# A second level of the seven-product form in four products of a tiled MLP, with its factors made in flight and streamed in 256 KB pieces

## The chip, the cores and the metric

One core of a Trainium2 chip runs the whole program in one launch. The metric is the device time in microseconds (us), smaller is better. Engines are named as in the profile: PE (TensorE, matmuls), DVE (VectorE), ACT (ScalarE), POOL (GpSimd), SP (SyncE). POOL and SP are used here almost only to issue DMA transfers.

## The reference

Lightning attention (batch 4, 8 heads, 768 positions, head size 64), then an MLP on each of the 3072 tokens:

```python
# attention, by blocks of positions, with a decay per head (lam)
intra = ((qb @ kb.T) * Dmask) @ vb
inter = (qb * lam_pow) @ kv_state
out   = intra + inter
kv_state = lam_block * kv_state + (kb * rev_pow).T @ vb
# MLP: x is 3072 x 512, w_in 512 x 2048, w_out 2048 x 512
h = x @ w_in
g = h - tanh(h)
return g @ w_out
```

Everything is fp32. The MLP dominates the arithmetic.

## The kernel before

**Groups.** The tokens are taken in six groups of 512: 128 positions of each of the four batches. The state of the attention runs from group to group. For each group there are two halves of attention work (batches 0, 1 and 2, 3), each with the steps `att_transpose` (L252), `att_scores` (L273), `att_out` (L309) and `att_state` (L287). At the end `att_sums` (L337) makes the sums of x that the MLP needs. From group 1 on, the attention of group g+1 runs in pieces between the products of group g, so that its waits lie beside TensorE work.

**Group 0** runs the MLP plainly (`up_plain` L481, `down_plain` L496) while the weights come in and are rounded (`round_block` L218). With each block of w_out `sums_out` (L207) forms seven factors from its four quadrants on DVE, and POOL stores them to a DRAM tensor `factors` (L215, L216), eight pairs of stores in all; the last is issued at 153.87 us.

**Groups 1 to 5** use the seven-product form of Strassen and Winograd: a product of two matrices, each cut in quadrants, is made of seven half-size products and some sums instead of eight. In the first stage, `up(g, u, n)` (L392) does product n of a quarter u (0 to 3) of the 2048 hidden columns, four matmuls of 128x256 each; its factors sit in SBUF. `evict` (L367) combines the products with ACT copies and DVE additions, and applies tanh. In the second stage, `down(g, n)` (L434) does product n over the whole hidden dimension, 16 matmuls of 128x256, with a factor of w_out of 1 MB that is streamed from `factors`. `load_factor` (L424) issues that load on POOL's queue, two products ahead, into a ring of two 1 MB buffers (pool `wst`, tag `w`).

**Order.** The main loop (L548 to L569) is an order written out by hand: for each u products 2, 6, 5, 7, then the next u's product 1 (or product 1 of the second stage after the last), then 4 and 3. In the second stage 2, 6, 5, 7, then the next group's first product, 4, 3. The first-half attention steps stand among u = 2, u = 3 and the second stage's product 2; the second half's stand after products 6, 5 and 7. Each engine takes its instructions in order, so a DVE operation that waits holds back those written after it; some operations are pinned with `keep_in_program_order`, and a scheduler places the others by what they need. Product 3 of the last group is split in three so that the end is short (L444 to L451).

**Loads on SP.** For groups 2 and up, q and k are loaded as blocks that DVE can transpose (L146): for each of the eight tiles, q and k of four batches, 16 transfers of 16 KB, hence 128 a group, into eight buffers of the pool `late`. k and v are loaded also in natural order (L125, `load_natural`), 256 KB each. These loads are issued a group ahead of use, as soon as their buffers are free; SP's queue holds them in the order q, k of batch 0, q, k of batch 1 and so on. The pool `late` is opened before group 1 in place of the staging pool of the weights (L546, L547).

**Stores.** The results of a group leave by four stores of 256 KB on POOL's queue (L476).

[...]

Of the kernel before, what the change touches and what calls it, by code (L numbers as in the profile page):

```python
# [16 lines left out]
BLK = 128  # L17
# [6 lines left out]
def kernel(  # L24
# [48 lines left out]
    wst = ctx.enter_context(tc.tile_pool(name="wst", bufs=2))  # L73
# [3 lines left out]
    gpool = ctx.enter_context(tc.tile_pool(name="gpool", bufs=NU))  # L77
# [3 lines left out]
    stage_open = tc.tile_pool(name="stage", bufs=1)  # L81
    stage = stage_open.__enter__()
# [37 lines left out]
    def load_natural(g, b, names):  # L120
        for name, src, bufs in (("q", q, 2), ("v", v, 4), ("k", k, 3)) if (g, b) == (0, B - 1) else (
                ("q", q, 2), ("k", k, 3), ("v", v, 4)):
            if name in names:
                x = io.tile([128, H, D], F32, name=f"{name}_nat", tag=name, bufs=bufs)
                nc.sync.dma_start(out=x, in_=src[b, :, ts(g, BLK), :].rearrange("h s d -> s h d"))  # L125
                raw[g, b][name] = x

    def load(n):

        while at["loaded"] < min(n, len(chunks)):
            g, b = chunks[at["loaded"]]
            if g < GB:
                raw[g, b] = {}
                load_natural(g, b, "qkv")
                at["loaded"] += 1
                continue
            for b in range(B):
                raw[g, b] = {}  # L140
                for name, src in (("q", q), ("k", k)):
                    x = late["pool"].tile([128, NP, BLK // 32, 32], F32, name=f"{name}_blk", tag="blk", bufs=2 * B)
                    for p in range(NP):
                        for c in range(4):
                            blk = src[b, 2 * p + c // 2, ts(g, BLK), ts(c % 2, 32)]
                            nc.sync.dma_start(out=x[ts(c, 32), p], in_=blk.rearrange("(r t) a -> t r a", t=32))  # L146
                    raw[g, b][name + "b"] = x
            for b in range(B):
                load_natural(g, b, "kv" if g < NG - 1 else "v")
            at["loaded"] += B  # L150
# [207 lines left out]
    def product_bank(key, n):  # L358

        if n == 1:  # L360
            banks[key, "y"] = bank("y", "y", 2)
# [5 lines left out]
    def evict(key, n, dst, finish):  # L367

        y, z, w = (banks.get((key, x)) for x in "yzw")
        end = key == ("down", NG - 1)  # L370
        halves = [slice(0, 256), slice(256, 512)] if end else [slice(None)]
# [7 lines left out]
        elif n == 7:  # L379
            for x in halves:  # L380
                nc.scalar.activation(dst(22)[:, x], y[:, x], AF.Copy)  # L381
            nc.vector.tensor_tensor(dst(22), dst(22), z, op=AL.add)  # L382
            finish(22, dst(22))
            if end:
                nc.vector.tensor_tensor(dst(12), dst(12), z, op=AL.add)
# [6 lines left out]
    def up(g, u, n):  # L392
        a, bname = FACT[n]
        wt = {"A11": w1[u][:, 0:2, 0], "A12": w1[u][:, 2:4, 0], "S3": w1[u][:, 0:2, 1], "A22": w1[u][:, 2:4, 1],
              "S1": ws[u][:, 0], "S2": ws[u][:, 1], "S4": ws[u][:, 2]}[a]
        x = xt[g][bname] if bname != "B11" else xt[g, 0][:, 0:2]
        t, first = product_bank(("up", g, u), n)
        for m in range(2):
            for kt in range(2):
                nc.tensor.matmul(out=t[:, m, :], lhsT=wt[:, kt, ts(m, 128)], rhs=x[:, kt, :],  # L400
                                 start=first and m == 0 and kt == 0, stop=kt == 1, skip_group_check=True)

        def dst(c):
            if (g, u, c) not in hid:
                hid[g, u, c] = gpool.tile([128, 2 * HB], F32, name=f"g{c}", tag=f"g{c}")
            return hid[g, u, c]

        def finish(c, src):
            th = work.tile([128, 2 * HB], F32, name="th", tag="th")
            nc.scalar.activation(th, src, AF.Tanh)  # L410
            nc.vector.tensor_tensor(dst(c), src, th, op=AL.subtract)  # L411

        evict(("up", g, u), n, dst, finish)
        if n == 3:

            hid[g, u, "S1"] = gpool.tile([128, 2 * HB], F32, name="gs1", tag="gs1")
            nc.vector.tensor_tensor(hid[g, u, "S1"], dst(12), dst(22), op=AL.add)
            nc.vector.tensor_tensor(dst(12), dst(11), dst(12), op=AL.subtract)

    ORDER = (1, 2, 6, 5, 7, 4, 3)  # L420
    stream = [(g, n) for g in range(1, NG) for n in ORDER]
    sent = {"n": 0}

    def load_factor(n):  # L424

        while sent["n"] < min(n, len(stream)):
            key = stream[sent["n"]]
            blks[key] = wst.tile([128, KH, 256], F32, name="wb", tag="w")
            nc.gpsimd.dma_start(out=blks[key], in_=factors[XAT[FACT[key[1]][1]]])  # L429
            sent["n"] += 1  # L430

    HIDAT = {"A11": 11, "A12": 21, "A22": 22, "S1": "S1", "S2": 11, "S3": 12, "S4": 21}

    def down(g, n):  # L434
        load_factor(stream.index((g, n)) + 2)
        wb = blks.pop((g, n))
        c = HIDAT[FACT[n][0]]

        def hidden(kt, m):
            return hid[g, kt // 2, c].rearrange("q (m c) -> q m c", m=2)[:, kt % 2, ts(m, 128)]  # L440

        if g == NG - 1 and n == 3:

            rows = out.rearrange("(b s) d -> s b d", b=B)[ts(g, BLK), 0:2, 256:512]  # L444
            for tag, bufs, m, c0, c1 in (("w", 1, 0, 0, 256), ("z", 1, 1, 0, 128), ("y", 2, 1, 128, 256)):
                t = bank("end", tag, bufs)[:, 0:c1 - c0]
                for kt in range(KH):
                    nc.tensor.matmul(out=t, lhsT=hidden(kt, m), rhs=wb[:, kt, c0:c1], start=kt == 0, stop=kt == KH - 1)  # L448
                o = hid[g, 12].rearrange("q (m c) -> q m c", m=2)[:, m, c0:c1]
                nc.vector.tensor_tensor(o, o, t, op=AL.add)  # L450
                nc.sync.dma_start(out=rows[:, m, c0:c1], in_=o)  # L451
            return
        t, first = product_bank(("down", g), n)
        for m in range(2):
            for kt in range(KH):
                a = hidden(kt, m)
                nc.tensor.matmul(out=t[:, m, :], lhsT=a, rhs=wb[:, kt, :], start=first and m == 0 and kt == 0,  # L457
                                 stop=kt == KH - 1, skip_group_check=True)
        if n == 2:
            for u in range(NU):  # L460
                nc.vector.tensor_tensor(hid[g, u, 11], hid[g, u, "S1"], hid[g, u, 11], op=AL.subtract)
            for u in range(NU):
                nc.vector.tensor_tensor(hid[g, u, 21], hid[g, u, 21], hid[g, u, 11], op=AL.subtract)

        def dst(c):
            if (g, c) not in hid:
                hid[g, c] = opool.tile([128, 512], F32, name=f"o{c}", tag="o")
            return hid[g, c]

        def finish(c, src):  # L470
            i, j = divmod(c - 11, 10)
            if src is not dst(c):
                nc.vector.tensor_copy(dst(c), src)
            rows = out.rearrange("(b s) d -> s b d", b=B)[ts(g, BLK), 2 * i:2 * i + 2, ts(j, 256)]
            o = dst(c).rearrange("q (m c) -> q m c", m=2)
            nc.gpsimd.dma_start(out=rows, in_=o)  # L476

        evict(("down", g), n, dst, finish)


    def up_plain(u, c):  # L481
        a, t = divmod(c - 11, 10)
        h = bank("h", *(("y", 2) if t == 0 else ("z", 1) if a == 0 else ("w", 1)))
# [5 lines left out]
        th = work.tile([128, 2 * HB], F32, name="th", tag="th")  # L489
        nc.scalar.activation(th, h, AF.Tanh)  # L490
        hid[0, u, c] = gpool.tile([128, 2 * HB], F32, name=f"g{c}", tag=f"g{c}")
        nc.vector.tensor_tensor(hid[0, u, c], h, th, op=AL.subtract)
# [3 lines left out]
    def down_plain(kt):  # L496
        wt = pair[kt]
        for b in range(B):
            if kt == 0:
                obank[b] = bank("op0", *((("y", 2), ("y", 2), ("z", 1), ("w", 1))[b]))  # L500
            i, t = divmod(b, 2)
            for a in range(2):
                g = hid[0, kt // 2, 11 + i + 10 * a].rearrange("q (m c) -> q m c", m=2)[:, kt % 2, ts(t, 128)]
# [42 lines left out]
    stage_open.__exit__(None, None, None)  # L546
    late["pool"] = ctx.enter_context(tc.tile_pool(name="late", bufs=8))  # L547
    up(1, 0, 1)  # L548
    for g in range(1, NG):
        last = g == NG - 1  # L550
        p0, p1 = attention(g + 1) if not last else ([], [])
        for u in range(NU):
            for n in (2, 6, 5, 7):
                up(g, u, n)
            if u + 1 < NU:
                up(g, u + 1, 1)
            else:
                down(g, 1)
# [4 lines left out]
        for n, more in ((2, p0[2:]), (6, p1[0:1]), (5, p1[1:2]), (7, p1[2:])):  # L563
            down(g, n)
            run(more)
        if not last:
            up(g + 1, 0, 1)
        down(g, 4)
        down(g, 3)  # L569
# [30 lines left out]
```

## Time and profile before

| what | us |
|---|---|
| median of 3 runs | 692.55 (691.5 to 692.83) |
| profiled execution, its own time | 693.28 |
| its span, first to last instruction | 691.4 |
| DVE, ACT, POOL busy | 353.2, 167.9, 55.8 |
| product 2 of the first quarter starts at (groups 1 to 4) | 157.65, 266.83, 376.00, 485.18 |
| a group, first to first | 109.2 |
| POOL, 35 factor loads of 1 MB, issue to landing (median) | 5.7 |
| POOL, 19 stores of 256 KB, issue to landing (median) | 5.5 |

The profile is one execution. "Span" lies between its first and last instruction. A busy share is of the span. The "chain that ended last" is followed back from the last instruction, at each step to what released it; a time on it is time that the kernel could be shorter only if that piece were shorter, or its cause. Each line of a chain has a start, a duration, an engine, the tile that is written, the source line and the count of instructions. An issue line of a queue has a start, a duration, and the number of transfers; a bracket behind it is a wait and what ended it. A matmul in fp32 leaves two records. Matmuls' names are those of the program's tiles: `wb` a streamed factor, `g` hidden values, `sp` scores, `kv` the state's update, `op` attention's output.

### The profile page before, as it was taken

Reading aid. Unit: us, or ns where it says so; the run is one execution under the profiler, and the core shown is the slowest. Engines: PE = TensorE matmul, PEld = TensorE weight load, DVE = VectorE, ACT = ScalarE, POOL = GpSimd, SP = SyncE. Lnnn points to the kernel's source line nnn. Section 1 sums busy time; section 2 is a strip of 40 time slices with the busy share of each in tenths; the row PEclk is TensorE's granted clock in tenths of the full one; section 3 lists DMA queues with packets and bytes.
Section 4 is the critical chain, followed back from the end, with each engine's and each line's share of the span. In section 5 each row is a group of like instructions: output and inputs, shape, how many; then the busy total and the mean of one; then the engine's idle time right before and its main releaser. Section 6 shows DMA issues by size and latency. Waiting matters only on the chain.

```text
span 691.4 us, 10409 instructions
## 1 busy us (share of the span) xinstructions
PE 678.4 (98%) x4112; PEld 569.2 (82%) x4112; DVE 353.2 (51%) x608; ACT 167.9 (24%) x283; POOL 55.8 (8%) x96
## 2 busy tenths in 40 slices
PE   6899999999999999999999999999999999999998
PEld 5688855558888888888888888888888888888887
DVE  3798756993467332566441446713446712254501
ACT  2665433323321011331010332000332101233100
POOL 0001212120001001000111000001000001000101
PEclk9999999999999999999999999999999999999999
DMA  9869948556227646263655803455600332400342
GB/s 188 215 201 252 286 151 242 180 167 172 35 33 178 163 131 180 34 112 92 169 170 141 157 1 87 104 163 175 159 1 1 131 129 80 149 1 0 100 159 106
DMA packets 144143, 89.82 MB, mean 130 GB/s; under 512 B 129824, under 2 KB 130208, under 8 KB 139616
## 3 DMA queue, kind: packets, MB, share of 16 engines
q0 software_dynamic: 11232, 58.46, 24.7%
q1 hardware_dynamic: 132720, 30.71, 23.2%
q8 instruction: 32, 0.52, 0.3%
q14 instruction: 15, 0.12, 0.1%
q10 hardware_dynamic: 144, 0.00, 0.0%
HBM read 75.50 MB, written 13.63 MB: 129 GB/s over the span
## 4 chain that ended last, share of the span: by engine, by line
PE 94%; DMA 3%; DVE 2%; ACT 0%; issue 0%; SPq 0%; ACTq 0%; DVEq 0%
PE y L457 20%; PE y L400 20%; PE z L400 10%; PE z L457 9%; PE op L504 8%; PE h L487 6%; PE w L457 5%; PE w L400 5%; PE sp L280 3%; PE op L331 3%; DMA raw<-in_moe_w_in_dram 2%; PE op L325 1%; PE kv L300 1%; PE tp L265 1%; PE end L448 1%; DMA q_nat<-in_q_dram 1%
## 5 line engine op out<-in xcount | busy, mean ns | idle before, releaser
L457 PE MATMUL y<-wb,g 128*128 128x256 f32 x640 | 142.3, 380 | 0.7 <-ACT o L381 0.7
L457 PEld LDWEIGHTS y<-wb,g 128*128 128x128 f32 x640 | 120.9, 190 | 18.1 <-ACT o L381 1.1
L400 PE MATMUL y<-xt,w 128*128 128x256 f32 x320 | 73.6, 380 | 0.0
L410 ACT ACTIVATE th<-g 128x512 f32<-128x512 f32 x60 | 37.8, 630 | 140.7 <-DVE g L375 86.1
L400 PEld LDWEIGHTS y<-xt,w 128*128 128x128 f32 x320 | 60.5, 190 | 8.9 <-issue 0.6
L411 DVE TENSOR_TENSOR g<-g,th 128x512 f32<-128x512 f32 x60 | 41.4, 690 | 32.5 <-ACT th L410 32.5
L429 POOL DMA_DIRECT2D wb<-factors x35 | 19.0, 543 | 481.0 <-PE y L457 364.9
L487 PE MATMUL h<-xt,w 128*128 128x256 f32 x256 | 56.2, 381 | 0.9 <-DVE w L237 0.9
L284 DVE TENSOR_TENSOR ss<-sp,mask 128x512 f32<-128x512 f32 x48 | 30.8, 684 | 51.4 <-PE sp L280 51.4
L504 PE MATMUL op<-wt,g 128*128 128x512 f32 x128 | 56.5, 595 | 0.0
L487 PEld LDWEIGHTS h<-xt,w 128*128 128x128 f32 x256 | 48.3, 190 | 8.3 <-DVE w L237 1.3
L504 PEld LDWEIGHTS op<-wt,g 128*128 128x128 f32 x128 | 23.8, 190 | 27.7 <-issue 27.0
L382 DVE TENSOR_TENSOR g<-g,z 128x512 f32<-128x512 f32 x20 | 13.7, 686 | 49.9 <-ACT g L381 49.9
L400 PE MATMUL y<-tt,ws 128*128 128x256 f32 x160 | 37.8, 379 | 0.0
L400 PE MATMUL w<-xt,w 128*128 128x256 f32 x160 | 37.8, 379 | 0.0
L400 PE MATMUL z<-tt,ws 128*128 128x256 f32 x160 | 37.8, 379 | 0.0
L400 PE MATMUL y<-tt,w 128*128 128x256 f32 x160 | 37.8, 379 | 0.0
L400 PE MATMUL z<-xt,ws 128*128 128x256 f32 x160 | 37.8, 379 | 0.0
L457 PE MATMUL w<-wb,g 128*128 128x256 f32 x160 | 35.8, 382 | 0.0
L457 PE MATMUL z<-wb,gs 128*128 128x256 f32 x160 | 35.3, 379 | 0.0
L400 PEld LDWEIGHTS y<-tt,ws 128*128 128x128 f32 x160 | 30.4, 190 | 4.1
L400 PEld LDWEIGHTS z<-xt,ws 128*128 128x128 f32 x160 | 30.4, 190 | 4.1
(92 smaller groups left out, 844.9 us busy)
## 6 DMA issues: line engine op xcount, KB each, us to landing
wb<-factors POOLq DMA_DIRECT2D x35, 1024.0 KB, 5.7
raw<-in_moe_w_out_dram POOLq DMA_DIRECT2D x16, 512.0 KB, 5.0
v_nat<-in_v_dram SPq DMA_DIRECT2D x24, 256.0 KB, 5.0
factors<-wt POOLq DMA_DIRECT2D x8, 768.0 KB, 5.4
k_nat<-in_k_dram SPq DMA_DIRECT2D x20, 256.0 KB, 5.0
out_dram<-o POOLq DMA_DIRECT2D x19, 256.0 KB, 5.5
raw<-in_moe_w_in_dram SPq DMA_DIRECT2D x8, 512.0 KB, 5.7
raw<-in_moe_w_in_dram SPq DMA_DIRECT2D x16, 256.0 KB, 4.6
```

What stands on the lines that cost most here:

```text
L265: nc.tensor.transpose(out=tp[:, p, :], in_=t[x][:, 2 * p:2 * p + 2, :], identity=ident)
L280: nc.tensor.matmul(out=sp[j][:, p, :], lhsT=kt[ts(j, 64), p, :], rhs=qt[ts(j, 64), p, :], start=True, stop=True)
L284: nc.vector.tensor_tensor(ss[:, j], sp[j], mask[:, j], op=AL.mult)
L331: nc.tensor.matmul(out=dst(n, p, j), lhsT=vn[:, 2 * p + j, :], rhs=ss[:, j, p, :], start=g == 0 and n == 0 and p % 2 == 0, stop=n == 1 and ...
L382: nc.vector.tensor_tensor(dst(22), dst(22), z, op=AL.add)
L400: nc.tensor.matmul(out=t[:, m, :], lhsT=wt[:, kt, ts(m, 128)], rhs=x[:, kt, :], start=first and m == 0 and kt == 0, stop=kt == 1, skip_gro ...
L410: nc.scalar.activation(th, src, AF.Tanh)
L411: nc.vector.tensor_tensor(dst(c), src, th, op=AL.subtract)
L429: nc.gpsimd.dma_start(out=blks[key], in_=factors[XAT[FACT[key[1]][1]]])
L457: nc.tensor.matmul(out=t[:, m, :], lhsT=a, rhs=wb[:, kt, :], start=first and m == 0 and kt == 0, stop=kt == KH - 1, skip_group_check=True)
L487: nc.tensor.matmul(out=hm[:, m, :], lhsT=w1[u][:, i, a, ts(m, 128)], rhs=xt[0, t][:, i, :], start=m == 0 and i == 0, stop=i == KI - 1, ski ...
L504: nc.tensor.matmul(out=obank[b], lhsT=g, rhs=wt[:, 2 * a:2 * a + 2, :], start=kt == 0 and a == 0, stop=kt == KH - 1 and a == 1)
```

## The change

Four of the seven products of the second stage (4, 5, 7 and 3; in the last group not 3, nineteen in all) are again done by the seven-product form, one level down. `down_twice` does one such product as seven subproducts, each of four matmuls of 128x128: 28 matmuls of half the columns in place of 16. Its left factors are sums of the hidden values, three 512-column DVE sums per product (`sums_twice`) and one more after subproduct 2; the seven partial results are copied from PSUM by ACT and added by DVE. The products' order is now 1, 2, 4, 6, 5, 7, 3.

The right factors of the subproducts are made once, in group 1: for each of the four products POOL loads the four quadrants of its factor (`load_quarters`, 256 KB each), DVE makes four differences, and POOL stores seven pieces of 256 KB to a DRAM tensor `fine` (`factors_twice`): 16 loads, 16 DVE operations and 28 stores.

All factors, those of products 1, 2 and 6 too, are streamed in pieces of 256 KB through a ring of seven buffers (`piece`, tag `wb`) in place of two of 1 MB. The quadrants of group 1 use the same ring. `down` goes over u outside, and over m and kt inside.

Around this: the hidden values of a group lie in one tile for all u; the two `y` banks become `ya` and `yb`; the block tiles of q and k have seven buffers instead of eight, and SP's order is q0, k0, q1, k1, q2, k2, q3, natural loads of batches 0 and 1, k3, natural loads of 2 and 3. The pools `wst`, `stage` and the early q tiles are closed before group 1, and `late`, opened after, holds blocks, ring, sums and partial results.

```diff
+    SUB = (1, 2, 6, 5, 7, 3, 4)
+    TWICE = (4, 5, 7, 3)
+    fine = dram.tile([len(TWICE), len(SUB), 128, NU, 128], F32, name="fine")
+    RING = 7
+    def twice(g, n):
+        return n in TWICE and not (g == NG - 1 and n == 3)
+    stream = [(g, n, x) for g in range(1, NG) for n in (1, 2, 4, 6, 5, 7, 3)
+              for x in (SUB if twice(g, n) else range(NU))]
...
+    def load_quarters(n):
+        for i in range(2):
+            for j in range(2):
+                quarters[n, i, j] = late["pool"].tile([128, NU, 128], F32, name="wq", tag="wb", bufs=RING)
+                factor_block(quarters[n, i, j], XAT[FACT[n][1]], i, j)
+    def factors_twice(n):
+        b11, b12, b21, b22 = (quarters.pop((n, i, j)) for i in range(2) for j in range(2))
+        t1, t2, t4 = (late["pool"].tile([128, NU, 128], F32, name=f"wt{x}", tag="sums", bufs=4) for x in (1, 2, 4))
+        for dst, x, y in ((t1, b12, b11), (t2, b22, t1), (b12, b22, b12), (t4, b21, t2)):
+            tc.keep_in_program_order(nc.vector.tensor_tensor(dst, x, y, op=AL.subtract))
+        for i, t in enumerate((b11, b21, t2, t1, b12, b22, t4)):
+            nc.gpsimd.dma_start(out=fine[TWICE.index(n), i], in_=t)
+    def piece(g, n, x):
+        i = stream.index((g, n, x))
+        while sent["n"] < min(i + RING, len(stream)):
+            g_, n_, x_ = stream[sent["n"]]
+            t = late["pool"].tile([128, 2, 256], F32, name="wb", tag="wb", bufs=RING)
...
+    def sums_twice(g, n):
+        a11, a12, a21, a22 = quarter(g, n)
+        s1, s2 = (late["pool"].tile([128, NU, 128], F32, name=f"s{x}", tag="sums", bufs=4) for x in (1, 2))
+        nc.vector.tensor_tensor(s1, a21, a22, op=AL.add)
+        nc.vector.tensor_tensor(s2, s1, a11, op=AL.subtract)
+        nc.vector.tensor_tensor(a21, a11, a21, op=AL.subtract)
+        low[g, n] = (s1, s2)
+    def down_twice(g, n, zw):
+        a11, a12, a21, a22 = quarter(g, n)
+        s1, s2 = low.pop((g, n))
+        y = bank("y2", "yb", 1)[:, 0:128]
+        zw = bank("zw", zw, 1)
+        o = res[g, n] = otile(f"q{n}")
+        r5 = late["pool"].tile([128, 128], F32, name="r5", tag="r5", bufs=2)
+        for x, a, dst, keep in ((1, a11, y, o[:, 0:128]), (2, a12, zw[:, 0:128], None), (6, s2, y, o[:, 128:256]),
+                                (5, s1, zw[:, 128:256], r5), (7, a21, y, o[:, 384:512]), (3, a12, zw[:, 128:256], None),
+                                (4, a22, y, o[:, 256:384])):
+            wb = piece(g, n, x).rearrange("p m c -> p (m c)")
+            for u in range(NU):
+                nc.tensor.matmul(out=dst, lhsT=a[:, u, :], rhs=wb[:, ts(u, 128)], start=x in (1, 2) and u == 0,
+                                 stop=u == NU - 1, skip_group_check=True)
+            if keep is not None:
+                nc.scalar.activation(keep, dst, AF.Copy)
+            if x == 2:
+                nc.vector.tensor_tensor(a12, a12, s2, op=AL.subtract)
+        nc.vector.tensor_tensor(o[:, 384:512], o[:, 384:512], r5, op=AL.add)
+        nc.vector.tensor_tensor(o[:, 0:256], o[:, 0:256], zw[:, 0:256], op=AL.add)
...
-    stage_open.__exit__(None, None, None)
-    late["pool"] = ctx.enter_context(tc.tile_pool(name="late", bufs=8))
+    early.close()
+    late["pool"] = ctx.enter_context(tc.tile_pool(name="late", bufs=1))
     up(1, 0, 1)
     for g in range(1, NG):
         last = g == NG - 1
         p0, p1 = attention(g + 1) if not last else ([], [])
         for u in range(NU):
+            if g == 1:
+                load_quarters(TWICE[u])
             for n in (2, 6, 5, 7):
                 up(g, u, n)
+            if g == 1:
+                factors_twice(TWICE[u])
             if u + 1 < NU:
                 up(g, u + 1, 1)
             else:
...
-        for n, more in ((2, p0[2:]), (6, p1[0:1]), (5, p1[1:2]), (7, p1[2:])):
-            down(g, n)
-            run(more)
+        sums_twice(g, 4)
+        down(g, 2)
+        run(p0[2:])
+        sums_twice(g, 5)
+        down_twice(g, 4, "z")
+        run(p1[0:1])
+        sums_twice(g, 7)
+        down(g, 6)
+        run(p1[1:2])
+        down_twice(g, 5, "w")
+        if not last:
+            sums_twice(g, 3)
+        run(p1[2:])
+        down_twice(g, 7, "z")
         if not last:
             up(g + 1, 0, 1)
-        down(g, 4)
-        down(g, 3)
+            down_twice(g, 3, "z")
+        else:
+            down_end(g)
```

## The prediction, made before the changed kernel ran

> **What bounds the kernel now.** I read the page's busy line first, then the chain of work that ended last, then that chain piece by piece, and only then the queues. The busy line and the chain agree:
>
> ```profile
> PE 678.4 (98%) x4112; PEld 569.2 (82%) x4112; DVE 353.2 (51%) x608; ACT 167.9 (24%) x283; POOL 55.8 (8%) x96
> ```
>
> ```profile
> PE 94%; DMA 3%; DVE 2%; ACT 0%; issue 0%; SPq 0%; ACTq 0%; DVEq 0%
> ```
>
> TensorE is busy for 98% of the span and is 94% of the chain, at the full granted clock in every slice. Only fewer TensorE seconds shorten this kernel, and any new TensorE wait lengthens it one for one. The price of a product is at the chain's end:
>
> ```profile
> 666.75 6.92 PE y L457 x32
> ...
> 673.69 0.38 ACT o L381
> ...
> 674.40 7.17 PE y L457 x32
> 681.57 7.04 PE end L448 x48
> ```
>
> The trace has two records for each fp32 matmul: a product of 16 matmuls of 128x256 takes 6.91 us in 32 records, 215.9 ns each. L448 mixes shapes: 16 records of 128x256 (3.45 us) and 32 of 128x128, which get the other 3.58 us: 111.7 ns each. That is the price of the new form.
>
> The second reading is SP's queue, idle on the chain but close to it. Its block loads for group 2, 16 DMAs a line:
>
> ```profile
> 145.56 7.45 SPq L146 DMA_DIRECT2D q_blk<-in_q_dram  x16
> 153.05 12.57 SPq L146 DMA_DIRECT2D k_blk<-in_k_dram  x16
> ...
> 205.99 9.49 SPq L146 DMA_DIRECT2D k_blk<-in_k_dram  x16
> ```
>
> They start at 145.56, while group 0 still runs, and their last lands shortly after 215.5. The matching POOL lines:
>
> ```profile
> 153.87 0.84 POOL L216 DMA_DIRECT2D factors<-wt  x1 [1.62 <-DVE wt L213]
> ...
> 158.75 0.54 POOL L429 DMA_DIRECT2D wb<-factors  x1 [1.35 <-DMA factors<-wt]
> ```
>
> The last store of the factors is issued at 153.87 and the first factor load waits for it until 158.75.
>
> **What the Trainium skill says.** "TensorE: Matmul & The Clock Gate", section "Back-to-back issue gap": the spacing in a stream of weight load and matmul is set by both, so halving a matmul's columns doesn't halve its time. The trace agrees: 111.7 against 215.9 ns, 3.4% above half. "DMA: Bandwidth & Descriptors", section "Issuing engines are not separate DMA queues": transfers issued by different engines share the same DMA engines. The trace agrees: comparing the starts of SP's block loads with POOL's transfers in flight, they start 0.51 us apart with none in flight, 0.65 with one, 0.79 with two. The same page, "Anatomy of one DMA — SWDGE (gpsimd) path", fits about 2.0 us plus bytes/436e3 us, 2.6 us for 256 KB as an estimate. The trace's 1 MB loads take a median of 5.7 us where the fit has 4.4, and the 256 KB stores of `o` 2.6 to 6.8, median 5.5; so I take 3 to 4.5 us for a 256 KB piece.
>
> **The change part by part.**
>
> *Products.* Four products in groups 1 to 4 and three in group 5 are 28 matmuls of 128x128 instead of 16 of 128x256: 56 × 0.1117 = 6.255 us for 6.91, 0.654 saved each. Nineteen give 12.4 us. Instruction counts on TensorE's queue rise (28 for 16), and so do semaphore instructions there, 80 to 166 at about 51 ns; they are nothing as long as the queue runs ahead of the array, as it does before (its drain stands at 686.44 while matmuls run to 688.6).
>
> *DVE.* Per group the second level adds three 512-column sums (0.69 us busy, starting every 0.60) for each of four products, merge adds, and a12−=s2. DVE works 23 of 55 us in a second stage, so throughput is there; position is not. Between up 3 and kv, DVE already runs without a gap:
>
> ```profile
> 216.86 0.68 DVE L461 TENSOR_TENSOR g<-gs,g 128x512 f32<-128x512 f32 x1
> ...
> 220.91 0.68 DVE L375 TENSOR_TENSOR o<-o,w 128x512 f32<-128x512 f32 x1
> 221.51 1.29 DVE L295 TENSOR_TENSOR k_nat<-k_nat,mask 128x512 f32<-128x512 f32 x2
> ```
>
> In the changed program's order three sums for product 4 and three for product 5 come into this stretch; counted in program order, twelve operations at 0.60 end the k_nat products at about 223.6 to 224.1 on this clock, where TensorE asks for them at 223.03. That is 0.65 us in each of groups 2 to 4: 1.95 in all, bounded by 0 (if the sums find earlier gaps) and 1.1 each.
>
> *ACT.* Five copies of 128 columns in each second-level product; the copy of 512 takes 0.60 us and of 256 0.38, so about 0.27 as an estimate on that line. They are needed before the bank is reused by the next subproduct but one; slack about 0.4 us. Nothing, at worst 0.2 each, 3.8 in all. ACT is at 4.6 us of 55 there, which hides them.
>
> *The end.* The 0.7 us before product 3 in the last group (ACT o L381 above) goes, since the product before it writes other banks; a similar hand-over, about 0.5, appears between products 5 and 7 (the same bank `y2`). Net −0.25.
>
> *Pieces.* Factors come as 256 KB in a seven-slot ring. In steady state a piece has 5.3 to 8 us from the slot's release to its use, against a landing of 3 to 4.5: 0 to 0.5 us a group; I take 0.5 over the kernel. A gain is excluded, as no TensorE wait on a factor stands in the chain before.
>
> *Group 1, the costly place.* There POOL loads 16 quarters and stores 28 fine factors of 256 KB, 11.5 MB in about 46 us, beside the pieces. Three waits meet. First, the pool that holds SP's block tiles now lies over the memory of `wst`, so in the built program the first block load waits for the landing of the last store of factors: about 158.4 instead of 145.6. Queued behind it on SP are all 128 block loads and the natural ones. Second, they then run beside POOL's traffic. The bounds are the rows for none and two in flight, 0.51 and 0.79. I take 0.75 us per load for the first 64 (between the rows of one and two in flight) and 0.63 for the next 64 (none and one). So k of batch 1 is issued by 158.4 + 48.0 and lands at about 210, in time for the scores of the first half at 211. k of batch 3 lands at 158.4 + 48.0 + 40.3 + 3.5 = 250.2; 0.67 for its transposes and 1.0 for the second half of its scores give 251.9. Before:
>
> ```profile
> 238.07 2.06 PE L280 MATMUL sp<-qt,kt 64*128 64x128 f32 x32
> ```
>
> ends at 240.1. So TensorE stands 11.9 us later there, with product 4's gain already inside. Third, POOL's own chain: a ring slot is reused only when a fine store has landed, so pieces for products 1 and 2 may be 1 to 6 us late near 200 and 213, and DVE's backlog adds about 4 at kv. These lie before the wait for k of batch 3 and are swallowed by it; they cost only if that wait is short. At 0.55 a load and below, the blocks are in time and 3 us of these remain; at 0.79 with landings of 5.5, the loss is 17 to 22.
>
> *Sum.* +11.9 (group 1) −18 × 0.654 (= −11.8; the nineteenth is inside the 11.9) + 1.95 + 0.5 − 0.25 = +2.3. The profiled execution took 693.28 (span 691.4 and 1.9 outside), so 695.6. The median of the runs shown is 0.73 below it: 694.9.
>
> **The rivals.** *A, the forecast*: SP's blocks late in group 1, 694.9.
> *B, blocks keep pace* (faster): POOL's small transfers disturb SP less than its 1 MB ones, 0.55 or less each, so blocks end by 158.4 + 70 + 3.5 = 232, before use. For it: 0.51 is the pace alone, and POOL often waits for DVE. Against: the table by transfers in flight. Group 1 then loses 3 for POOL's chain and DVE: 692.55 − 12.4 + 3 + 1.95 + 0.5 − 0.25 = 685.4.
> *C, all is hidden* (faster): only the saving and the end remain: 692.55 − 12.65 = 679.9. For it: DVE at 51%. Against it: the late start of the block loads is in the program.
> *D, POOL's chain in group 1 sets the time* (slower): a load waits for a store's landing, a store for DVE, DVE for k's transposes, and these for SP. With landings at the 5.5 of the `o` row in place of 3.5 and a pace of 0.79 to 0.75, scores end at 262, +22: 692.55 + 22 − 11.8 + 2.2 = 705. It decides from a pace of about 0.75 over all 128.
> *E, pieces late in every product* (slower): with landings above 5.3 us a piece misses its use; 1 us in each of 19 products on top of B would be 704.
> That the change doesn't shorten the products is excluded only as far as 111.7 ns holds for a product of 28 alone; at 120 ns 19 products would save 3.6 instead of 12.4. I give it no case of its own.
>
> **How the numbers follow.** Chances: A 0.50, B 0.27, C 0.06, D 0.12, E 0.05. A measurement of this kernel tells 0.2%, 1.4 us, from no change. A alone spans 688 to 701 (pace of the second half 0.53 to 0.69, DVE 0 to 1.1 a group); of its 0.50 I put 0.10 below 691.1, 0.10 within and 0.30 above 693.9. Faster is then 0.27 + 0.06 + 0.10 = 0.43, the same 0.10, slower 0.30 + 0.12 + 0.05 = 0.47. The range is 682.0 to 704.0: it leaves out C, about 0.07 of D, 0.03 of E and 0.02 of B, 0.18 together. As cases of both signs hold most of the chance: the likeliest one's own range is 688 to 701.
>
> **What would show it.** In the profile after: rows of 128x128 at 56 records and 6.25 us for each second-level product (111.7 ns; if not, the saving is mis-sized). SP's first block load at about 158 and not 146; k of batch 3 landing near 250; a TensorE wait of some 10 us before the second scores of group 1 released by DVE transposes behind that DMA. If TensorE has no gap there, A is wrong and B or C holds; if the gap's releaser is a `wb` piece, D or E. In groups 2 to 4, waits of about 0.65 us before kv, released by DVE k_nat. The prediction is wrong if block loads stay at 0.55 beside POOL, or if a stall of the steady groups, four times repeated, exceeds 1 us.

## The result and the profile after

The changed kernel takes 692.66 us (median of 4 runs, 691.6 to 693.51), the kernel before 692.45 (4 runs): the ratio is 1.0004, with a 95% interval of 0.9987 to 1.0022. This measurement can't tell it from no change. The profiled execution of the changed kernel took 692.45 us, its span is 690.6.

The page after, busy line and chain by engine:

```profile
PE 671.1 (97%) x4568; PEld 576.1 (83%) x4568; DVE 428.3 (62%) x747; ACT 191.0 (28%) x372; POOL 170.0 (25%) x302
```

```profile
PE 84%; issue 6%; DMA 5%; POOL 3%; DVE 1%; ACT 1%; POOLq 0%
```

TensorE is busy for 7.3 us less, but where it had 94% of the chain it has 84%: the chain now leaves it for POOL, DMA and stretches without a visible releaser. POOL's issue time has tripled.

The saving is there, and of the size that was forecast. The chain of the last group shows a subproduct as a line of 8 records and a product at one level as a line of 32:

```profile
657.64 0.89 PE y L539 x8
658.53 0.89 PE zw L539 x8
659.43 0.89 PE y L539 x8
660.32 6.91 PE y L496 x32
```

Seven times 0.893 are 6.25 us where one product at one level takes 6.91.

Where it was lost is read from the length of each group, the distance between the first rows of product 2 in two groups (first quarter, tile `w`) in the timeline of TensorE. (The starts listed for the kernel before come from the view of the chain, which puts each 0.17 us later than the timeline; the lengths are the same.) Four products at two levels should make a group 109.18 − 4 × 0.654 = 106.56 us long.

| group | before | after | expected | after less expected |
|---|---|---|---|---|
| 1 | 109.2 | 118.1 | 106.6 | +11.5 |
| 2, 3 (each) | 109.2 | 107.5 | 106.6 | +0.9 |
| 4 | 107.3 | 104.7 | 104.7 | 0.0 |
| 5, to the end of the span | 99.1 | 97.1 | 97.1 | 0.0 |

So almost all of it is in group 1. The sum closes: −12.4 for nineteen products, +11.5, +1.8, and −1.7 because group 1 began at 155.75 instead of 157.48 us in this execution, make −0.8, which is the difference of the spans. (The last 1.7 is no effect that we ascribe to the change: the kernels below share the first group's code, and their starts lie between 155.5 and 157.8.)

The timeline of TensorE in group 1 (start, duration, and in brackets the idle time before and its releaser):

```profile
198.65 1.89 PE L393 MATMUL y<-xt,w 128*128 128x256 f32 x8
206.84 9.78 PE L496 MATMUL y<-wb,g 128*128 128x256 f32 x32 [6.30 <-issue]
216.45 1.89 PE L393 MATMUL y<-tt,w 128*128 128x256 f32 x8
```

Product 1 of the second stage begins 6.3 us late and then takes 9.78 us instead of 6.91. The page's row of the granted clock has an 8 in that slice, and the table by stretches (start and end, length, the busy times of PE, PEld, DVE, ACT and POOL, then the granted clock, the DMA share and GB/s) shows it closer:

```profile
206.80:216.70 9.90, 9.87 (x34) 8.28 (x35) 5.40 (x9) 0.05 (x1) 3.78 (x8) 0.73 0.48 113
```

The first twelve records of the product follow each other at 0.43 us, the later ones at 0.216: TensorE ran at half its clock for 5.3 us after the wait. The Trainium skill has this under "TensorE: Matmul & The Clock Gate", Part 1 (the HAM clock gate): idle time puts the clock to half, sustained work restores it. The trace agrees in the ratio, 0.43 to 0.216. The wait costs 6.3 + 2.9 = 9.2 us.

Who is late is read from POOL's queue just before:

```profile
187.76 2.25 POOL L444 DMA_DIRECT2D wq<-factors  x3
190.96 0.75 POOL L444 DMA_DIRECT2D wq<-factors  x1 [0.96 <-DMA fine<-wq]
193.22 0.56 POOL L461 DMA_DIRECT2D fine<-wq  x1 [1.51 <-DMA wq<-factors]
...
199.33 0.76 POOL L444 DMA_DIRECT2D wq<-factors  x1
200.08 1.08 POOL L473 DMA_DIRECT2D wb<-factors  x2
203.16 0.54 POOL L473 DMA_DIRECT2D wb<-factors  x1 [2.00 <-DMA fine<-wq]
```

The pieces of product 1 (`wb`, L473) stand behind the loads of the last making's quarters (`wq`) and stores of the third and the last making (`fine`). Those loads wait for slots, a slot is free when a fine store has landed, and the stores wait for loads and for DVE. The first piece is issued at 200.08, when TensorE is 0.5 us from needing it, and lands at 206.50; product 1 starts at 206.84. So the wait that the profile puts down to "issue" is one for a piece.

What the prediction had put first is here too, but behind that wait. SP's queue and DVE:

```profile
156.53 10.41 SPq L136 DMA_DIRECT2D q_blk<-in_q_dram  x16
...
232.88 7.54 SPq L136 DMA_DIRECT2D k_blk<-in_k_dram  x16
```

```profile
245.55 0.71 DVE L271 STREAM_TRANSPOSE kt<-k_blk 128x512 f32<-128x512 f32 x1 [3.16 <-DMA q_blk<-in_q_dram]
```

```profile
247.21 2.06 PE L291 MATMUL sp<-qt,kt 64*128 64x128 f32 x32
```

SP starts at 156.5 and not at 146. The last k tile lands at 245.42 and is transposed at 245.55 (the bracket names a q load, but the tile that is read is k's). TensorE, 9 us late by then, runs the scores at 247.21 without a gap. Without the earlier wait it would have stood there for some 7 us, an estimate that takes the same landing: the second half of the scores would have been due near 239.

### The profile page after: what moved, and what is told of

It is laid out like the page before. It is cut to its first block, busy times and chain, and to the rows that moved or that the text cites. A ratio compares the mean times of both kernels' runs of the same rounds, so it can differ in the third digit from the quotient of the medians.

```text
span 690.6 us, 12075 instructions
## 1 busy us (share of the span) xinstructions
PE 671.1 (97%) x4568; PEld 576.1 (83%) x4568; DVE 428.3 (62%) x747; ACT 191.0 (28%) x372; POOL 170.0 (25%) x302
## 4 chain that ended last, share of the span: by engine, by line
PE 84%; issue 6%; DMA 5%; POOL 3%; DVE 1%; ACT 1%; POOLq 0%
PE y L393 16%; PE y L496 10%; PE y L539 10%; PE z L393 8%; PE h L579 8%; PE zw L539 7%; PE w L496 5%; PE op L595 4%; PE w L393 4%; PE sp L291 3%; DMA wq<-factors 3%; PE op L342 3%; POOL fine L461 1%; PE kv L311 1%; PE op L336 1%
## 5 line engine op out<-in xcount | busy, mean ns | idle before, releaser
L470 POOL DMA_DIRECT2D wb<-fine x133 | 71.5, 538 | 135.6 <-PE w L496 44.3
L473 POOL DMA_DIRECT2D wb<-factors x64 | 34.7, 544 | 208.5 <-PE y L496 180.3
L496 PE MATMUL y<-wb,g 128*128 128x256 f32 x320 | 73.4, 390 | 6.3 <-issue 6.3
L496 PEld LDWEIGHTS y<-wb,g 128*128 128x128 f32 x320 | 62.3, 196 | 15.3 <-issue 6.7
L542 ACT ACTIVATE q<-y 128x128 f32<-128x128 f32 x76 | 21.1, 277 | 99.3 <-PE y L539 99.3
L539 PE MATMUL y<-wb,g 128*128 128x128 f32 x336 | 45.3, 278 | 0.0
L539 PEld LDWEIGHTS y<-wb,g 128*128 128x128 f32 x336 | 41.2, 192 | 1.1 <-issue 0.3
```

Of the source, the lines that this page charges most:

```text
L470: nc.gpsimd.dma_start(out=t.rearrange("p m c -> p (m c)"), in_=fine[TWICE.index(n_), SUB.index(x_)].rearrange("p u c -> p (u c)"))
L473: nc.gpsimd.dma_start(out=t, in_=factors[XAT[FACT[n_][1]]][:, 2 * x_:2 * x_ + 2, :])
L496: nc.tensor.matmul(out=t[:, m, :], lhsT=a[:, u, kt, ts(m, 128)], rhs=wb[:, kt, :], start=first and u == 0 and m == 0 and kt == 0, stop=u = ...
L539: nc.tensor.matmul(out=dst, lhsT=a[:, u, :], rhs=wb[:, ts(u, 128)], start=x in (1, 2) and u == 0, stop=u == NU - 1, skip_group_check=True)
L542: nc.scalar.activation(keep, dst, AF.Copy)
```

## The experiments

The theory after the traces: in group 1 the making of the fine factors delays several things at once, and the wait that comes first in time hides those behind it. The first is POOL's queue (9.2 us at product 1), the next SP's k of batch 3. The rivals: SP's late blocks alone (as recorded); POOL's queue order alone; the second level itself costs more than its records.

Lengths of group 1 below are read as in the table; "over" is over 106.56 us.

**1. Nothing is made.**

```diff
-            if g == 1:
-                load_quarters(TWICE[u])
...
-            if g == 1:
-                factors_twice(TWICE[u])
...
-                                    in_=fine[TWICE.index(n_), SUB.index(x_)].rearrange("p u c -> p (u c)"))
+                                    in_=factors[XAT[FACT[n_][1]]][:, 2 * (x_ % 4):2 * (x_ % 4) + 2, :].rearrange(
+                                        "p m c -> p (m c)"))
```

> Left out: the making of the fine factors in group 1 (16 loads, 16 DVE operations, 28 stores); the second-level products read 256 KB pieces of the coarse factors instead, so their values are not the reference's while every size stays. Theory (two chains in a row in group 1: POOL's queue makes the first pieces of product 1 late by 6.3 us and the half clock after it costs 2.9 more; right behind it SP's block loads, whose last k landed at 245.5 us where it would be wanted near 239): both go with the traffic, 692.7 - 9.2 - 1.1 = about 682 (680 to 684), no TensorE gap near 200 us, granted clock 1.00. Rival (the second level itself, its copies, sums and small pieces, costs more than the records show in every group): 688 or more.

684.38 us (682.76 to 685.05), ratio to before 0.9886 (0.9868 to 0.9904): 0.4 above the expected range, and well below the rival's 688. Group 1 is 107.5 us long, 0.9 over, the same as groups 2 and 3. Between 158 and 200 us the DMA share is 0.37 where the changed kernel has 0.89. What is left in the waits of TensorE from group 1 on is one line:

```profile
PE kv L311 <- PE op L342: 1.8, 3, 0.6
```

The second level and its streaming are thus worth what was reckoned; the making costs 10.6 us of group 1. The rival of a dear second level falls.

**2. SP early alone.** The block tiles get a pool over the staging memory.

```diff
+    late["blk"] = ctx.enter_context(tc.tile_pool(name="blk", bufs=1))
...
-                x = late["pool"].tile([128, NP, BLK // 32, 32], F32, name=f"{name}_blk", tag="blk", bufs=2 * B - 1)
+                x = late["blk"].tile([128, NP, BLK // 32, 32], F32, name=f"{name}_blk", tag="blk", bufs=2 * B - 1)
```

(and `stage` is opened ahead of `wst`, so that it lies under the new pool)

> Only the block tiles move: they get a pool of their own over the staging memory, so that SP's first block load for group 2 starts at about 146 us, as in the kernel before, and not at 156.5. Theory of two chains: the wait of 6.3 us for product 1's pieces and the half clock stay, since POOL's queue is unchanged; 692 (691 to 694). Rival, the recorded forecast (SP's blocks set the loss in group 1): the loss of about 9 us goes, 683 to 685.

692.5 us, ratio 0.9997 (0.9987 to 1.0007). SP starts as wanted, and the wait stays:

```profile
144.79 7.45 SPq L136 DMA_DIRECT2D q_blk<-in_q_dram  x16
```

```profile
PE y L496 <- issue: 6.2, 1, 6.2
```

Group 1 is 118.5 us long. SP's late start is not what this kernel loses by, as long as the wait for product 1's pieces stands ahead of it.

**3. Three of the four makings.**

```diff
-            if g == 1:
+            if g == 1 and u < NU - 1:
                 load_quarters(TWICE[u])
...
-            if g == 1:
+            if g == 1 and u < NU - 1:
                 factors_twice(TWICE[u])
...
-                                    in_=fine[TWICE.index(n_), SUB.index(x_)].rearrange("p u c -> p (u c)"))
+                                    in_=fine[TWICE.index(7 if n_ == 3 else n_), SUB.index(x_)].rearrange("p u c -> p (u c)"))
```

> Left out: the making of product 3's fine factors (4 of 16 quarters, 7 of 28 stores); product 3 reads those of product 7, so its values are wrong and its time is not. SP's late start stays. Theory of two chains: product 1's pieces are issued near 190 instead of 200 us, so the wait near 200 goes (-9.2), but TensorE then stands 4 to 7 us before the second half of the scores, for k of batch 3: 687 to 690. Rival (POOL's queue alone is the cause): no wait takes its place, 683.

683.42 us (682.35 to 684.52), ratio 0.9881 (0.9861 to 0.99): the rival's number. Group 1 is 109.0 us long. POOL's queue and TensorE:

```profile
188.05 1.09 POOL L473 DMA_DIRECT2D wb<-factors  x2
```

```profile
200.01 7.07 PE L496 MATMUL y<-wb,g 128*128 128x256 f32 x32
```

The pieces are asked for 12 us earlier. The k tile that we expected to be late was transposed at 237.91, not 245.55, and the scores waited for nothing:

```profile
237.91 0.71 DVE L271 STREAM_TRANSPOSE kt<-k_blk 128x512 f32<-128x512 f32 x1 [4.93 <-DMA q_blk<-in_q_dram]
```

With a quarter of the making its traffic was gone too. Up to 200 us that made no difference (DMA share 0.87 between 158 and 200 us against 0.89; SP's fifth tile starts at 199.13 against 198.89), but SP's last three tiles took 24.9 us to issue instead of 29.4. So this edit took away two things at once, and doesn't tell a queue's order from the bytes.

**4. Both edits.**

> The two edits before together (product 3 again reads product 7's fine factors, which leaves out a quarter of the making). Theory of two chains: both waits go, 682 to 684, and the gain of the pair (about 9) is more than the sum of the single ones (0 and 3 to 6). Rival (one cause alone): equal to the better of the two single edits within 1 us.

684.22 us (683.29 to 685.13): within 1 us of the third run, as the rival said. The k tiles were early, but nothing was gained by it: the natural k load of batch 3 came late, and one of the k_nat products with it:

```profile
250.35 0.69 DVE L306 TENSOR_TENSOR k_nat<-k_nat,mask 128x512 f32<-128x512 f32 x1 [4.42 <-DMA k_nat<-in_k_dram]
```

So to tell order from bytes, the bytes have to stay, as they do in the next three experiments.

**5. The bytes without the buffers.** Added to the third run:

```diff
+            elif g == 1:
+                for i in range(7):
+                    nc.gpsimd.dma_start(out=fine[3, i].rearrange("p u c -> p (u c)"),
+                                        in_=factors[i][:, 0:2, :].rearrange("p m c -> p (m c)"))
```

> Three factors made as in the run of that name (product 3 reads product 7's fine factors, so its values are not the reference's), but the bytes of the fourth making are moved all the same: seven copies of 256 KB from DRAM to DRAM on POOL's queue in the fourth quarter of group 1, which no buffer and no DVE operation waits for. Theory A (order in POOL's queue is the cause, not the bytes): within 1.5 us of the run without the copies, 683 to 685. Theory B (the bytes slow everything; with them k of batch 3 lands near 243 and the scores wait): 687 to 690.

683.85 us (683.63 to 686.68). This run tells nothing: nothing held the copies in their place, and the scheduler put them at 79.8 to 91.4 us, in group 0. The next has `in_=fine[1, i]` as their source.

> As the run with the copies, whose copies the scheduler had moved into group 0, so that it told nothing: now they read the fine factors of product 5, which exist from about 190 us, and so lie in group 1 (product 3 reads product 7's fine factors, as before). Theory A (order in POOL's queue, not bytes): 683 to 685.5. Theory B (bytes): k of batch 3 lands some 3 to 5 us later than in the run without copies and the scores wait: 687 to 690.

688.66 us (686.33 to 689.51), ratio 0.9941 (0.9923 to 0.9958), the number of theory B, but not at B's place. Group 1 is 112.2 us long. The copies lie between 176 and 198 us. The scores don't wait; the loss is earlier, where DVE's differences wait for the delayed quarters and an addition that TensorE needs stands behind them:

```profile
187.68 2.53 PE L393 MATMUL z<-tt,ws 128*128 128x256 f32 x8 [2.63 <-DVE g L419]
```

After this wait 8 records again ran at half clock. But the run doesn't tell bytes from order either, since the copies themselves stand on POOL's queue:

```profile
176.20 0.53 POOL L652 DMA_DIRECT2D fine<-fine  x1 [0.33 <-issue]
...
194.67 1.48 POOL L652 DMA_DIRECT2D fine<-fine  x3 [2.49 <-DMA fine<-wt]
```

The quarter that DVE waited for is issued 1.0 us later after the start of group 1 than in the third run, behind the first copy, and lands 5.55 us after its issue instead of 4.85: of the 1.7 us, 1.0 is place in the queue and 0.7 a slower landing. Later a copy held the queue for 2.49 us, because it waited for product 5's stores.

**6. The whole making, in another order.** Product 1's pieces ahead of the last quarters, the last differences at the end of the first stage:

```diff
             if g == 1:
+                if u == NU - 1:
+                    ahead(NU)
                 load_quarters(TWICE[u])
...
-            if g == 1:
+            if g == 1 and u + 1 < NU:
                 factors_twice(TWICE[u])
...
+        if g == 1:
+            factors_twice(3)
         sums_twice(g, 4)
```

(`ahead(n)` is the loading part of `piece`, up to the n-th piece of the stream)

> The changed kernel with all its making in group 1, the same transfers, but in another order on POOL's queue: product 1's four pieces are asked for ahead of the fourth quarter's loads, and the fourth making stands on DVE ahead of the second stage's sums. Theory (order and slots in POOL's queue cost the 9.2 us, not the bytes): the wait near 200 us goes; a rest of 1 to 4 us for the fourth making stays, later in group 1: 683.5 to 687. Rival (the bytes of the making are too many for group 1, so the wait only moves): 690 or more, with SP's k of batch 3 landing near 245.

690.01 us (9 runs, 686.17 to 691.75), ratio 0.9962 (0.9944 to 0.998). In the profiled execution (691.2 us) group 1 is 115.3 us long, 2.8 us less than in the changed kernel. The first pieces are asked for at 188.10 and the wait near 200 us is gone, while the DMA share between 158 and 200 us is 0.89 as in the changed kernel: that wait came from the order and not from the bytes. The longest of TensorE's waits after 150 us show what came instead:

```profile
PE sp L291 <- DVE kt L271: 3.2, 1, 3.2
PE w L497 <- DMA wb<-factors: 2.1, 1, 2.1
PE y L497 <- DMA wb<-factors: 1.7, 1, 1.7
PE kv L311 <- issue: 1.3, 1, 1.3
```

The first is the wait of the prediction: k of batch 3, transposed at 244.44. The second is a piece of product 2 in group 1, the third one of product 6 in the last group, and the fourth is DVE's backlog before kv in group 1. The rival's number, and what it said: most of the wait only moves. SP's queue waits for nothing of POOL's here, so that k of batch 3 is transposed at 244.44 and not at 237.91, as in the third run, is what the fourth making's traffic does to SP's loads.

**7. The same with SP early.**

> The kernel with product 1's pieces ahead of the fourth quarter's loads, and beside that SP's block tiles in a pool of their own over the staging memory, so that the block loads start near 145 instead of 156.5 us; the whole making stays in group 1. Theory of two chains, one behind the other: the wait of 3.2 us for k of batch 3, which took the place of the wait near 200 us, goes too: 686 to 688, of which a natural k load of batch 3 may give 1 us back. Rival (k's wait is the price of the bytes alone, wherever SP starts): 690 as before.

689.21 us (22 runs, 686.15 to 695.14), ratio 0.9952 (0.9938 to 0.9966), short of the 686 to 688 that was expected, and by time not to be told from the sixth run. Group 1 is 114.1 us long in the profile. The wait for k is gone from the list, and another has come up:

```profile
PE w L497 <- DMA wb<-factors: 2.1, 1, 2.1
PE kv L311 <- issue: 1.5, 1, 1.5
...
PE kv L311 <- DVE k_nat L306: 1.0, 1, 1.0
```

Here the third line is the natural k load again, as in the fourth run.

**8. DVE's order before kv.** The sums for product 5 are pinned behind the k_nat products.

```diff
+            tt = nc.vector.tensor_tensor(dst, x, y, op=op)
+            if n == 5:
+                tc.keep_in_program_order(tt)
```

> The changed kernel with one difference: the three DVE sums for product 5 are pinned in program order, so they stand behind the k_nat products that kv waits for, where the scheduler had put them ahead. Theory (the 0.9 us that TensorE loses between product 2 and kv in each of groups 1 to 3 is this DVE backlog): kv follows attention's output without a gap, -1.8 to -2.7 against the changed kernel, 690 to 691. Rival (the gap is TensorE's own, as its inferred releaser says, a matmul): no difference, 692.5.

691.74 us (14 runs), ratio to before 0.9991 (0.9981 to 1.0001), above the 690 to 691 that was expected and too near to tell by time. The profile does tell. The changed kernel, then this one, in group 2:

```profile
337.58 1.97 PE L342 MATMUL op<-ss,v_nat 128*64 128x128 f32 x32
340.14 1.24 PE L311 MATMUL kv<-v_nat,k_nat 128*64 128x64 f32 x32 [0.59 <-PE op L342]
```

```profile
338.05 1.97 PE L342 MATMUL op<-ss,v_nat 128*64 128x128 f32 x32
339.85 1.10 PE L311 MATMUL kv<-v_nat,k_nat 128*64 128x64 f32 x32
```

The gap is gone and groups 2 and 3 last 106.56 us each, 0.91 less, exactly the length expected without waits. Group 1 stays at 118.1: the gap is gone there too, but in this execution the wait for DVE's differences in the third quarter is 1.9 us instead of 1.1. The releaser that the profile names (a matmul) had long been done; it was DVE, as the edit shows.

**9. Streaming alone.** All products at one level, nothing made, pieces and ring as changed.

> Only the streaming part of the change: every factor in 256 KB pieces through the seven slots, the new order of products and layout, but all products at one level and no fine factors made. Theory (pieces are hidden; all loss is in the making and in DVE's backlog): no TensorE wait on a piece, 691 to 693, the kernel before less at most the 0.7 us wait of its last group. Rival (small pieces cost something in every product, a tenth of a microsecond per piece or more): 140 pieces add several us, 695 or more.

691.73 us (14 runs), ratio 0.9987 (0.9978 to 0.9997). TensorE has no wait on a piece, and the 0.7 us before the last group's product 3 is gone. Streaming in 256 KB pieces costs nothing that shows, as this run's theory had it.

**10. A better version.** Three makings in group 1; product 3's in group 2, where POOL is free; product 3 at one level in group 1; product 5's sums pinned. The computation is whole.

```diff
-        return n in TWICE and not (g == NG - 1 and n == 3)
+        return n in TWICE and not (g in (1, NG - 1) and n == 3)
...
+            if stream[sent["n"]] == (2, 1, 0):
+                load_quarters(3)
...
+            if g == 2 and u == 0:
+                factors_twice(3)
+                cap["n"] = len(stream)
```

> A version with the whole computation: fine factors for products 4, 5 and 7 are made in group 1 as before, those of product 3 at the start of group 2, where POOL is free; product 3 stays at one level in group 1 (0.65 us more); the sums for product 5 are pinned behind k_nat as in the run before. Theory: 683.4 (three made) + 0.65 - 1.8 to 2.7 = 681.5 to 682.5, no TensorE wait near 200 us and none in group 2. Rival (wherever the last four quarters are made, the ring stalls the pieces): a wait of several us at the start of group 2's second stage, 686 or more.

683.29 us (682.62 to 683.6), ratio 0.9872 (0.9859 to 0.9885). Group 1 lasts 108.6 us, groups 2 and 3 106.56: the fourth making costs TensorE nothing in group 2. The 0.8 us above the expected range are accounted for by one late piece in the last group (1.8 us):

```profile
PE y L500 <- DMA wb<-factors: 1.8, 1, 1.8
```

The piece was issued between 645 and 647 and wanted at 649.7. The memory has room for an eighth slot.

> The version with product 3's making in group 2, with eight slots instead of seven in the ring. Theory (the 1.8 us that its profile lost before product 6 of the last group is a piece that had 5 us from slot to use): an eighth slot gives each piece 0.9 to 1.7 us more, the wait goes, 681.5 to 682.5. Rival (a late piece is late with eight slots too): 683.3 as with seven.

682.52 us (6 runs, 680.16 to 687.32), ratio 0.9867 (0.984 to 0.9894). In its profile (681.69 us) TensorE waits for no piece; from group 1 on, one wait of 0.5 us is left, and that is k of batch 3. The single runs scatter too much to say by time that the eighth slot helps. Both versions are faster than both kernels by some 9 to 10 us.

## Why the prediction was right or wrong

Its likeliest time, 694.9 us, lies 2.2 above the measured one, which is well inside its range. Its balance was right: nineteen products save 12.4 us and group 1 gives about as much back. Its story of how group 1 gives it back was not. By the signs that it named itself, case A did not come true: TensorE has no gap before the second scores, and the gap that stands is one for a `wb` piece, the sign of D or E. That the number came out is luck in this term.

- *Products*: 6.255 us each reckoned, 6.25 measured. Right: groups 4 and 5 have just the expected length.
- *Group 1*: 11.9 us late with one product's gain inside, so 12.6 lost; 11.5 measured (6.3 + 2.9 at product 1, 1.1 for DVE's differences in the third quarter, 0.9 at kv, and 0.3 that we don't place). The two sums agree by chance: 11.9 was worked out for one wait, and 11.5 is made of others. (By its own figures the prediction's wait is 251.9 − 240.1 = 11.8.)
- *Its cause*: the step that failed is "These lie before the wait for k of batch 3 and are swallowed by it". It was the other way round. The pieces' wait near 200 us, given as 1 to 6 us, was 6.3, and half clock added 2.9 that no step had priced; it came first in time, so it swallowed the wait for k. That tile landed about 5 us earlier than reckoned (it landed at 245.42; 250.2 was predicted), since the first load started at 156.5 instead of 158.4 and the first seven tiles went at 0.62 to 0.75 us a load, the eighth at 0.47. The pace of 0.79 with two of POOL's transfers in flight is not borne out by the trace before: over the loads for group 2 the mean is 0.50 with none (92 loads), 0.67 with one (21) and 0.68 with two or more (14), and the medians of the first two are 0.47: a few long steps make the means. Undoing SP's late start alone gave nothing (second run). Once the first wait was taken away with the bytes kept, the predicted wait appeared, at 3.2 us (sixth run).
- *Rival D* had the right queue, POOL's, and a loss of 22 us, twice too much. Its landings of 5.5 us were near for loads (between 156 and 220 us the quarters' median is 5.3), too long for the fine stores (4.1 from a quarter, 3.8 from a difference), but its size came from a pace of 0.75 to 0.79 for SP.
- *DVE before kv*: 0.65 us each in groups 2 to 4 predicted, 0.9 in groups 2 and 3 measured, none in group 4: the last group updates no state, so there is no kv. 1.95 against 1.8, two errors that cancel. The cause was right (eighth run).
- *The end, ACT, pieces*: about nothing, as reckoned. The 0.7 us wait went; two subproducts of the last product 7 took 1.08 us instead of 0.89, and one piece of the last product was 0.4 late. The pieces landed in 3.6 us (median of those from the fine factors) and 5.3 (from the coarse ones), where 3 to 4.5 were taken: the slack was smaller than reckoned, and the tenth experiment shows a piece that missed it.
- *The sum*: +2.3 predicted against −0.8 in the profiled executions. Of the 3.1, 1.1 is group 1, and 1.7 the earlier start of group 1, which is scatter of the first group.

What stays open: how the 10.6 us of the making split. Order on POOL's queue alone gives 2.8 back, order and an early SP 4.0 (each from one profiled execution), leaving a quarter of the making out 9.1. So the parts don't add: the makings delay POOL's pieces, SP's blocks and DVE at once, each wait hides the next, and of the edits tried only those that take making out of group 1 relieved it. Which of them would be last if only DVE's part were taken away wasn't tried.

## What to carry to other kernels

When work that is done once is squeezed into one stage, look for all the queues that it delays there, not for the latest one by the forecast: the wait that comes first in time hides the rest, and taking it away alone gives back only the difference to the next (2.8 of 10.6 us here). Moving a part of such work to a stage with a free queue, at the price of running one product the old way once, brought group 1 from 118.1 to 108.6 us (with the pinned sums). And a transfer for the near future belongs ahead of transfers for the far future on an in-order queue, above all where the latter wait for slots: with the pieces asked for first, the wait of 6.3 us was gone.

## What the hardware did that was not expected

A TensorE wait of 6.2 to 6.4 us was followed by 4 to 5.3 us at half clock in all three kernels that had it, which made it cost 8.3 to 9.2 us. Of shorter waits, one of 2.6 us (8 records at half speed, after five at full) had a like effect, while waits of 1.8, 2.1 and 3.2 us had none. So a wait's price can be more than its length, and these runs show no fixed length from which it is. What they show is the stretch at half clock itself: it lasted 6.8 us in the three kernels (from 205.33 to 212.16 in the changed one) and 3.4 in the fourth, and began 3.5 to 4.8 us after TensorE had fallen idle, in the fourth when work had been back for 1.3 us. Only the part of the stretch in which there is work costs time, about half its length (2.9 us for 5.3 in the changed kernel). In the changed kernel SP's 16 KB loads went at 0.47 us each in the eighth tile (7.54 us for 16, at a DMA share of 0.65) and at 0.62 to 0.75 in the first seven (share 0.69 to 0.97); the kernel before had 0.79 in one tile (12.57 us for 16).
